# Retention without projections in between, a plain chunk of 256 tokens and passes of 512, output weights kept split

## Chip, cores, metric

One core of a Trainium2 chip. The metric is device time in microseconds of one execution of the program; the runs of the kernel before have a median of 917.03 us (915.97 to 918.96, three runs).

## What is computed

Retention over 4 batches, 8 heads, 576 positions, head size 64, then two feed-forward layers over the 2304 tokens of width 512. The second and third weights arrive as 64-bit floats and are converted on the chip.

```python
scores = (1 / sqrt(64)) * (q @ k.T)            # per batch and head
ret = scores * where(i >= j, gamma[h] ** (i - j), 0.0)
x = (ret @ v)  # -> (2304, 512), heads side by side

g = x @ w_gate                 # 512 x 1536
x = (g / (1 + exp(-g))) * (x @ w_val) @ w_out     # w_out 1536 x 512

r = maximum(x @ w_in, 0.0)     # 512 x 2048
out = (r * r) @ w_out2         # 2048 x 512
```

## The kernel before

All activations stay in one SBUF tile `xy` (128 x 4 x 2304). A float32 product is made as three TensorE matmuls: each operand is split by `split` into a rounded part (ScalarE cast, names ending in `_h` or `hi`) and a remainder (VectorE subtraction, `_l` or `lo`), and hi*hi, hi*lo, lo*hi are summed in PSUM (`three`, `product`).

**Retention** runs over 16 pairs (batch, two heads), `n` = 0 to 15, plus two iterations that only finish (`LAG` = 2). An iteration does `scores(n)` (tile `s`, masked by VectorE into `p_sb` and `pl`), `states(n)` (`kvs`, then a chain of three VectorE operations on `sb`), and `apply(n - 2)` (`o`, copied by ScalarE into `xy`). While it runs, `chain["on"]` ties every instruction to the one before it on its engine, so the written order is the order on the engine.

**Weights** come in units of 128 x 512 values. `conversion` loads a unit (`raw`, 512 KB), and `words` turns it into `w` with two ScalarE and four VectorE operations (two TENSOR_SCALAR, one SCALAR_TENSOR_TENSOR, one addition that the profile names CUSTOM_DVE_ANT_0). `pump` advances it a step at a time, `ensure` runs it until a unit is there. Before, each unit is stored to DRAM (`wst`) and read back (`w_in`, `wo`) where it is needed. 14 units are converted during retention.

**First layer, before.** Tokens 0 to 447 (`M0`) are a plain chunk: gate and value of the first six blocks (`hidden0`, 12 matmuls of 448 columns each) stand one behind each retention iteration from `n` = 6 to 17, their output products (`out0`, 72 matmuls, banks `a`) stand at the start of the first pass, and blocks 6 to 11 of the chunk form a small pass of their own (`"rest"`, 144 + 72 matmuls of 448). The other 1856 tokens go through two passes of two 464-token blocks. There, a pair of weight blocks and a pair of token blocks is multiplied with seven products instead of eight (`slot`, i = 1 to 7): the stationary operands `wi` are sums and differences of weight quarters (`stationary`, on GpSimd, split by ScalarE and VectorE, stored as `win` in the first pass and loaded in later ones), the moving operands `xo` are sums and differences of token blocks (`renew`, in place in `xy`). A system is one such set of 7 x 6 = 42 matmuls; a pass of the first layer has 12 systems (gate `g` and value `v` of six block pairs) and 288 output matmuls (`out1`, bank `oacc`, summed into `xy` by VectorE).

**Second layer.** Three passes of two 384-token blocks, 8 systems each (336 matmuls of 384 columns), and `out2`, 288 matmuls of 512 columns a pass.

After retention the order on the engines is set by the scheduler of the compiler layer, not by the written order.

In the profile nearly every operation has line L116, the line of the wrapper that issues it, so tiles tell the operations apart. Operations that the text speaks of: `p_sb`, `pl` at lines 405, `sb` 425, `renew` 540, `out0` 313, `hidden0` 294, `load_out` 713, the main loop 797.

Of the kernel before, what the change touches and what calls it, by code (L numbers as in the profile page):

```python
# [21 lines left out]
P = 128  # L22
# [17 lines left out]
HALF = F1 // 2  # L40
FROM = 6

LAG = 2

WA = 14

WARM = 3
UNITS_EARLY = 14

PUMPS = {0: 1, "out": 4}  # L50

PACE = 1.1
# [9 lines left out]
def retention_moe_kernel(  # L62
# [23 lines left out]
    early, parts = ExitStack(), ExitStack()  # L86
    ctx.enter_context(parts)
    ctx.enter_context(early)
    wa_p = pool(parts, "wa_p", WA)
    xs_p = pool(early, "xs_p", 4)  # L90
    t_p = pool(early, "t_p", 2)
# [11 lines left out]
    class Chained:  # L103
# [5 lines left out]
        def __getattr__(self, name):  # L109
            op = getattr(self.engine, name)  # L110

            def traced(*args, **kw):
                with ExitStack() as behind:
                    if chain["on"] and self.last is not None:
# [11 lines left out]
    units = {}  # L126
    order = [(1, what, f) for f in range(HALF) for what in "gv"] + [(1, "o", f) for f in range(HALF)]
    plain = len(order)
    for k in range(HALF // 2, F1 // 2):
        order += [(1, what, f) for f in (2 * k, 2 * k + 1) for what in "gv"] + [(1, "o", 2 * k), (1, "o", 2 * k + 1)]  # L130
    for k in range(F2 // 2):
        order += [(2, what, f) for what in "io" for f in (2 * k, 2 * k + 1)]
    raw_t, raw_flat, w_t = {}, {}, {}
    spare = []
    loads = {"next": 0, "pool": 0, "open": False, "cap": len(order) - 1}

    def prefetch(upto):

        while loads["next"] <= min(upto, len(order) - 1):
            i = loads["next"]  # L140
            if loads["pool"] < 2:
                loads["pool"] += 1
# [14 lines left out]
    wst = {u: part_p.tile([P, 512], F32, tag="w{}{}{}".format(*u), name="wst") for u in order}  # L157
    stored = set()

    def weight_tiles():  # L160
        return [wa_p.tile([P, 512], F32R, tag=x, name=f"w_{x}") for x in ("hi", "lo")]

    def finish(i):
        wf = w_t.pop(i).bitcast(F32)
        if i < plain:
            hi, lo = weight_tiles()
            split(hi, lo, wf)
            units[order[i]] = (hi, lo)
        sp.dma_start(out=wst[order[i]], in_=wf)
        stored.add(order[i])  # L170

    def words(raw, back, flat):
# [5 lines left out]
        wt = cv_p.tile([P, 512], U32, tag="w", name="w", bufs=3)  # L178
# [21 lines left out]
    def conversion():  # L200
        for i in range(len(order)):
            prefetch(max(i, min(i + 3, loads["cap"])))
            raw, back = raw_t[i]
            for n, wt in enumerate(words(raw, back, raw_flat.pop(i, None))):
                w_t[i] = wt
                if n == 2:
                    if i:
                        finish(i - 1)
# [3 lines left out]
            if back is None:  # L212
                loads["pool"] -= 1
            elif loads["open"]:
                spare.append(back)
            yield
        finish(len(order) - 1)
        yield

    def split(hi, lo, src):  # L220
        act.copy(hi, src)
        dve.tensor_tensor(out=lo, in0=src, in1=f32(hi), op=ALU.subtract)

    def stationary(w0, w1_, s1, to):
# [6 lines left out]
        yield  # L231
        yield
# [14 lines left out]
    def pump(k=1):  # L247
        for _ in range(k):
            if pumped["n"] < pumped["limit"]:
                pumped["n"] += 1  # L250
                next(convert, None)

    def ensure(key, where):
        while key not in where:
            pumped["n"] += 1
            next(convert)

# [11 lines left out]
    def split_x(cc):  # L269
        src = xy[:, cc, :M0]  # L270
        hi = xs_p.tile([P, M0], F32R, tag="xh", name="xh")
        lo = xs_p.tile([P, M0], F32R, tag="xl", name="xl")
        split(hi, lo, src)
        xs[cc] = (hi, lo)
# [7 lines left out]
    def cut(pair, a, n):  # L282
        return tuple(x[:, a:a + n] for x in pair)

    def project(f, what):
# [6 lines left out]
    hs, gates = {}, {}  # L292

    def hidden0(k):

        f, what = divmod(k, 2)
        ps = project(f, "gv"[what])
        yield
        if what == 0:
            gates[f] = t = t_p.tile([P, M0], F32, tag="t", name="t")  # L300
            act.activation(out=t, in_=ps, func=AF.Silu)
            return
        t = gates.pop(f)
        dve.tensor_tensor(out=t, in0=ps, in1=t, op=ALU.mult)
        yield
        hi, lo = (x[:, :M0] for x in weight_tiles())
        split(hi, lo, t)
        hs[f] = (hi, lo)

    acc = []  # L310
    part = part_p.tile([P, CC, M0], F32, tag="part", name="part")

    def out0(f):

        if f == 0:
            acc.extend(ps_a.tile([P, 512], F32, tag=f"a{i}", name=f"a{i}")[:, :M0] for i in range(CC))
        ensure((1, "o", f), units)
        w, h = units.pop((1, "o", f)), hs.pop(f)
        for cc in range(CC):
            three(acc[cc], cut(w, cc * P, P), h, f == 0, f == HALF - 1)  # L320
        if f < HALF - 1:
            return
        for cc, a in enumerate(acc):
# [598 lines left out]
```

## Time and profile before

| | us |
|---|---|
| median of three runs | 917.03 |
| the profiled execution, device time | 920.45 |
| its span in the trace | 918.7 |
| TensorE busy | 884.8 |
| VectorE busy | 679.3 |
| ScalarE busy | 438.6 |
| GpSimd busy | 103.3 |

The trace is that of the profiled execution; its device time is 1.75 us over its span and 3.4 us over the median. A matmul's recorded duration includes its way through the array; the rate of a row of matmuls is read from the distance of their starts. Three stages follow each other: retention up to 120.1 us, the first layer up to about 520 us (its end overlaps the second layer's start), the second layer to the end.

### The profile page before, as it was taken

To read this page: it belongs to the slowest core of one execution; us is meant where nothing else is said; L and a number is where in the kernel's file an instruction comes from. 1 tells how busy PE (TensorE), PEld (TensorE's weight loads), DVE (VectorE), ACT (ScalarE), POOL (GpSimd) and SP (SyncE) were. 2 spreads that over 40 slices of the span, in tenths; PEclk is the share of its full clock that TensorE was granted. 3 is DMA by queue.
4 is the path that set the end of the run, shared out by engine and by line. 5 is a ranking of instruction groups with operands and counts; after the bars stand their busy time and mean duration, and the time that the engine had idled before them with its cause. 6 is when DMAs were issued, how large, how long until landed. Compare 5 with 4: busy or idle time off the path is not lost.

```text
span 918.7 us, 13809 instructions
## 1 busy us (share of the span) xinstructions
PE 884.8 (96%) x5050; PEld 782.0 (85%) x5050; DVE 679.3 (74%) x1098; ACT 438.6 (48%) x781; POOL 103.3 (11%) x119
## 2 busy tenths in 40 slices
PE   7899959899999999899999999999999999999998
PEld 6688848788888899788888999989999999998986
DVE  3777887879989998877877899668754568554553
ACT  3555555675656655455543547534433334243220
POOL 2121160323303000000000223200000000000000
PEclk9999989899999999999999999999999999999999
DMA  8888557998879757889985457534664454554402
GB/s 327 280 277 292 160 196 234 358 318 283 296 258 305 277 190 252 261 302 330 317 289 194 152 200 253 199 140 148 204 197 127 160 171 161 171 184 155 141 3 69
DMA packets 83076, 202.85 MB, mean 221 GB/s; under 512 B 8512, under 2 KB 20288, under 8 KB 83008
## 3 DMA queue, kind: packets, MB, share of 16 engines
q1 hardware_dynamic: 83008, 201.97, 65.3%
q8 instruction: 40, 0.66, 0.3%
q14 instruction: 28, 0.23, 0.1%
HBM read 141.77 MB, written 60.16 MB: 220 GB/s over the span
## 4 chain that ended last, share of the span: by engine, by line
PE 71%; DMA 11%; DVE 10%; issue 3%; ACT 3%; POOL 1%; SPq 1%; ACTq 0%; DVEq 0%; POOLq 0%
PE oacc L116 29%; PE g L116 20%; PE v L116 11%; DMA raw<-in_w 6%; PE z L116 4%; DVE w L116 3%; PE o L116 3%; PE s L116 3%; DVE wi L116 2%; DMA w_in<-wst 1%; DVE xy L116 1%; DMA wst<-w 1%; DMA win<-wi 1%; DVE xo_l L116 1%; DMA kv_sb<-in_kv 1%
## 5 line engine op out<-in xcount | busy, mean ns | idle before, releaser
L116 PE MATMUL g<-xo_h,wi 128*128 128x464 f32 (+2 forms) x816 | 251.1, 359 | 9.4 <-ACT wi L116 3.3
L116 PE MATMUL oacc<-wo,ho_hi 128*128 128x512 f32 x576 | 181.0, 392 | 0.0
L116 PEld LDWEIGHTS g<-xo_h,wi 128*128 128x128 f32 x816 | 153.6, 190 | 23.9 <-ACT cbg L116 4.0
L116 PE MATMUL g<-xo_l,wi 128*128 128x464 f32 (+2 forms) x408 | 146.1, 358 | 0.0
L116 PE MATMUL v<-xo_h,wi 128*128 128x464 f32 (+2 forms) x432 | 136.8, 359 | 7.9 <-ACT wi L116 5.3
L116 PE MATMUL oacc<-ho_hi,wo 128*128 128x464 f32 (+1 forms) x432 | 138.5, 372 | 0.5 <-DVE xy L116 0.5
L116 PEld LDWEIGHTS oacc<-wo,ho_hi 128*128 128x128 f32 x576 | 107.3, 188 | 17.6
L116 DVE TENSOR_TENSOR xy<-oacc,xy 128x464 f32<-128x464 f32 (+2 forms) x146 | 94.3, 650 | 33.8 <-PE oacc L116 33.6
L116 PE MATMUL oacc<-wo,ho_lo 128*128 128x512 f32 x288 | 112.6, 392 | 0.0
L116 PEld LDWEIGHTS v<-xo_h,wi 128*128 128x128 f32 x432 | 80.8, 189 | 15.5 <-ACT wi L116 5.7
L116 PEld LDWEIGHTS oacc<-ho_hi,wo 128*128 128x128 f32 x432 | 81.0, 188 | 10.1 <-DVE xy L116 0.9
L116 DVE TENSOR_SCALAR w<-w 128x512 f32<-128x512 f32 (+1 forms) x136 | 58.6, 431 | 37.2 <-ACT w L116 36.4
L116 PEld LDWEIGHTS g<-xo_l,wi 128*128 128x128 f32 x408 | 77.7, 191 | 6.4
L116 PE MATMUL oacc<-ho_lo,wo 128*128 128x464 f32 (+1 forms) x216 | 80.1, 371 | 0.0
L116 ACT ACTIVATE raw<-raw 128x512 uint32<-128x512 uint16 x68 | 45.9, 675 | 68.6 <-DMA raw<-in_w 62.8
L116 PE MATMUL v<-xo_l,wi 128*128 128x464 f32 (+2 forms) x216 | 77.2, 357 | 0.0
L116 DVE TENSOR_TENSOR wo<-wo 128x512 fp32r<-128x512 f32 x78 | 54.2, 708 | 16.5 <-ACT wo L116 16.3
L116 DVE TENSOR_TENSOR cbg<-v,cbg 128x384 f32<-128x384 f32 (+1 forms) x72 | 41.7, 579 | 30.1 <-ACT cbg L116 19.4
L116 PEld LDWEIGHTS oacc<-wo,ho_lo 128*128 128x128 f32 x288 | 54.1, 188 | 11.5
L116 ACT CAST wo<-wo 128x512 fp32r<-128x512 f32 x78 | 47.4, 622 | 32.5 <-DMA wo<-wst 31.7
L116 ACT CAST wi<-w_in 128x512 fp32r<-128x512 f32 x72 | 44.1, 618 | 38.2 <-POOL w_in L116 9.2
L116 PE MATMUL z<-xo_h,wi 128*128 128x464 f32 (+1 forms) x192 | 61.8, 360 | 0.2 <-DVE cag L116 0.2
(100 smaller groups left out, 1366.6 us busy)
## 6 DMA issues: line engine op xcount, KB each, us to landing
wi<-win SPq DMA_DIRECT2D x84, 512.0 KB, 4.2
raw<-in_w SPq DMA_DIRECT2D x68, 512.0 KB, 5.0
win<-wi SPq DMA_DIRECT2D x60, 512.0 KB, 4.3
wo<-wst SPq DMA_DIRECT2D x78, 256.0 KB, 4.2
wst<-w SPq DMA_DIRECT2D x68, 256.0 KB, 5.2
w_in<-wst SPq DMA_DIRECT2D x52, 256.0 KB, 4.1
qk_sb<-in_qk SPq DMA_DIRECT2D x15, 576.0 KB, 5.8
kv_sb<-in_kv SPq DMA_DIRECT2D x15, 576.0 KB, 4.4
```

Of the source, the lines that this page charges most:

```text
L116: i = op(*args, **kw)
```

## The change

- Retention holds no projections. Instead it prepares the first pass: the operands of the first system (`operands`, one step per iteration from `n` = 6) and five of its seven moving operands (`chunks`, from `n` = 10), and the split of the plain chunk (`split_x`). A VectorE remainder is issued some steps behind its ScalarE cast (`behind`, `catch_up`). 7 units are converted there, not 14.
- The first layer's passes are two of 2 x 512 tokens. The plain chunk is 256 tokens (1024 to 1279) and is computed inside the first pass: each system has two `plain_slot`s of 12 matmuls of 256 columns, whose stationary operands are the quarters that the system has anyway and one more (`wb`); `out1` for it has 24 matmuls of 256 columns per block pair. `"rest"`, `out0` and the round trip of its partial sums through DRAM are gone.
- Units of the first layer are no longer stored in DRAM and read back: up to five (`HOLD`) wait in SBUF. Output weights are split once and kept split in DRAM (`wsp`, 512 KB a unit), later passes load both parts; in the first layer GpSimd makes the remainder.
- The second layer's passes take neighbouring token blocks; its matmuls are the same.

```diff
-M0 = 448
-M = {1: 464, 2: 384}
+M0 = 256
+M1 = 512
+T0 = 2 * M1
...
-    (1, 0): (M0 + M[1], M0 + 2 * M[1]),
-    (1, "rest"): (0,),
-    (1, 1): (M0, M0 + 3 * M[1]),
-    **{(2, p): (M[2] * p, NT // 2 + M[2] * p) for p in range(NT // (2 * M[2]))},
+    (1, 0): (0, M1),
+    (1, 1): (T0 + M0, T0 + M0 + M1),
+    **{(2, p): (2 * M[2] * p, 2 * M[2] * p + M[2]) for p in range(NT // (2 * M[2]))},
...
-HALF = F1 // 2
-FROM = 6
...
-UNITS_EARLY = 14
-
-PUMPS = {0: 1, "out": 4}
-
-PACE = 1.1
+UNITS_EARLY = 7
+HOLD = 5
+
+PACE = {(1, 0): 1.3, (1, 1): 1.3, (2, 0): 1.3}
...
-        sp.dma_start(out=wst[order[i]], in_=wf)
-        stored.add(order[i])
+        if i in w_t:
+            sp.dma_start(out=wst[order[i]], in_=w_t.pop(i).bitcast(F32))
+            stored.add(order[i])
...
-        for i in range(len(order)):
+        for i, key in enumerate(order):
+            while loads["held"] > HOLD - 1:
+                yield "held"
...
+            if key[0] == 1:
+                ready[key] = wt.bitcast(F32)
+                loads["held"] += 1
+            else:
+                w_t[i] = wt
...
+    behind = []
+
+    def catch_up():
+        while behind:
+            lo, src, hi = behind.pop(0)
+            dve.tensor_tensor(out=lo, in0=src, in1=hi, op=ALU.subtract)
+
     def split(hi, lo, src):
         act.copy(hi, src)
-        dve.tensor_tensor(out=lo, in0=src, in1=f32(hi), op=ALU.subtract)
+        behind.append((lo, src, f32(hi)))
+        if not chain["on"]:
+            catch_up()
...
+        to(4, a21)
...
-        ensure((1, what, f), units)
-        ps, w = bank(what)[:, :M0], units.pop((1, what, f))
-        for cc in range(CC):
-            three(ps, cut(w, cc * P, P), xs[cc], cc == 0, cc == CC - 1)
-        return ps
...
+        inputs[n] = [xs_p.tile([P, max(512, 2 * M0)], F32, tag="x", name="w_in")[:, :512] for x in range(2)]
+        for x, w in enumerate(inputs[n]):
+            ensure((ph, what, 2 * k + x), stored)
+            sp.dma_start(out=w, in_=wst[ph, what, 2 * k + x])
...
+        def to(x, src):
+            if x == 4:
+                if ph == 1:
+                    built[n, "p"] = w = wb_p.tile([P, 2, 256], F32R, tag="p", name="wb")
+                    split(w[:, 0], w[:, 1], src)
+                return
+            w = operand_tile(n, x)
+            split(w[:, 0], w[:, 1], src)
+            later.append((win[ph, k, what, x], w.bitcast(F32)))
...
-            if last:
-                bank = s_t[min(n + LAG, len(pairs) - 1)][:, 0, 256:256 + D]
-            else:
-                bank = ps_o.tile([P, 512], F32, tag="o", name="o")
+            bank = ps_g.tile([P, 512], F32, tag="gv"[last], name="o")[:, :D if last else 512]
...
+        def operands():
+
+
+            yield 6
+            load_in(0)
+            for _ in build(0):
+                yield 6
+
+        def chunks():
+            for i, step in ((1, 1), (5, 0), (5, 1), (6, 0), (6, 1), (2, 1), (7, 0), (7, 1)):
+                yield LAG + 2 * NP
+                renew((1, 0), i, step)
+            for cc in range(CC):
+                yield LAG + 3 * NP
+                split_x(cc)
+
+        begun = [[x, next(x)] for x in (operands(), chunks())]
+
+        def begin(n, which):
+            catch_up()
+            x = begun[which]
+            if n >= x[1]:
+                x[1] = next(x[0], 99)
...
-            fill = PUMPS[0] if n >= FROM - 2 else 0
...
+            fill = int(n > 2)
+            pump(2 * fill)
             if old:
                 apply(n - LAG, False)
-            pump(fill)
-            if LAG < n <= LAG + CC:
-                split_x(n - LAG - 1)
+            begin(n, 1)
             if new:
                 scores(n, (NC - 1,))
             pump(fill)
+            begin(n, 0)
...
-            if n == last + LAG:
-                apply(n - LAG, True)
-            if FROM <= n < FROM + 2 * HALF:
-                for _ in hidden0(n - FROM):
-                    pass
-            if old and n < last + LAG:
+            if n % 2:
+                begin(n, 1)
+            else:
+                catch_up()
+            if old:
                 apply(n - LAG, True)
             if nxt:
...
+        for x, _ in begun:
+            for _ in x:
+                catch_up()
+        catch_up()
+        pump(5 * UNITS_EARLY)
...
     def plain_slot(n, r):
 
         ph, p, k, what = systems[n]
-        ps = bank("gv"[r])[:, :M0]
-        product(n, ps, True, *(((1, 1), (2, 2)), ((7, 1), (4, 2)))[r])
+        ps = out_bank()[:, :M0]
+        for cc in range(CC):
+            w = built[n, ((1, 2), ("p", 4))[r][cc // 2]][:, :, cc % 2 * P:][:, :, :P]
+            three(ps, (w[:, 0], w[:, 1]), xs[cc], cc == 0, cc == CC - 1)
         if what == "g":
             if r == 0:
...
+                sys_[n]["c"] = gate_p.tile([P, 2, M0], F32, tag="gate", name="gate")
...
+        gc = sys_[n - 1]["c"]
+        tt(out=gc[:, r], in0=ps, in1=gc[:, r], op=ALU.mult)
         if r:
-            hidden(n, "a", ga)
+            hidden(n, "c", gc)
...
+    def load_out(n, fs):
+        ph, p = systems[n][:2]
         for f in fs:
-            ensure((ph, "o", f), stored)
-            w = wo_p.tile([P, 2, 512], F32R, tag="wo", name="wo")
-            sp.dma_start(out=w[:, 1].bitcast(F32), in_=wst[ph, "o", f])
-            act.copy(w[:, 0], f32(w[:, 1]))
-            tt(out=w[:, 1], in0=f32(w[:, 1]), in1=f32(w[:, 0]), op=ALU.subtract)
-            wos[f] = w
+            key = (ph, "o", f)
+            w = wos[f] = wo_p.tile([P, 2, 512], F32R, tag="wo", name="wo")
+            if p:
+                sp.dma_start(out=w.bitcast(F32), in_=wsp[key])
+                continue
+            if ph == 1:
+                ensure(key, ready)
+                src = ready.pop(key)
+                loads["held"] -= 1
+                act.copy(w[:, 0], src)
+                pool_e.tensor_tensor(out=w[:, 1], in0=src, in1=f32(w[:, 0]), op=ALU.subtract)
+            else:
+                ensure(key, stored)
+                sp.dma_start(out=w[:, 1].bitcast(F32), in_=wst[key])
+                act.copy(w[:, 0], f32(w[:, 1]))
+                tt(out=w[:, 1], in0=f32(w[:, 1]), in1=f32(w[:, 0]), op=ALU.subtract)
+            sp.dma_start(out=wsp[key], in_=w.bitcast(F32))
```

The order on TensorE in a retention iteration. Before, from `n` = 6 on (of the 12 matmuls of a projection the first three stand here):

```order
L116 MATMUL s<-qk_sb 128x128 x8
L116 MATMUL o<-qs,sb 64x128 x6
L116 MATMUL o<-p_sb,kv_sb 64x128 x8
L116 MATMUL s<-qk_sb 64x64 x2
L116 MATMUL kvs<-kv_sb 64x64 x8
L116 MATMUL v<-xh,w_hi 128x448
L116 MATMUL v<-xl,w_hi 128x448
L116 MATMUL v<-xh,w_lo 128x448
```

After, the same iteration:

```order
L106 MATMUL s<-qk_sb 128x128 x8
L106 MATMUL o<-qs,sb 64x128 x6
L106 MATMUL o<-p_sb,kv_sb 64x128 x8
L106 MATMUL s<-qk_sb 64x64 x2
L106 MATMUL kvs<-kv_sb 64x64 x8
L106 MATMUL o<-qs,sb 64x64 x2
L106 MATMUL o<-pl,kv_sb 64x64 x2
```

The projection is gone from the iteration, and nothing stands in its place on this engine.

The order on VectorE in the same stage, one iteration from one `p_sb` on. Before (`w_lo` is a weight's remainder, `raw` and `w` are conversion steps):

```order
L116 TENSOR_TENSOR p_sb<-s,mask_sb 128x1024
L116 ISA w<-raw,w 128x1024
L116 TENSOR_SCALAR w<-w 128x512
L116 TENSOR_TENSOR pl<-s,mask_sb 64x128
L116 TENSOR_TENSOR w_lo<-w,w_hi 128x512
L116 TENSOR_SCALAR w<-w 128x512
L116 SCALAR_TENSOR_TENSOR sb<-sb,qs_sb,kvs 128x64 x3
L116 SCALAR_TENSOR_TENSOR w<-raw,w 128x512
```

After, the iteration `n` = 14, the one with the most in it:

```order
L106 TENSOR_TENSOR p_sb<-s,mask_sb 128x1024
L106 TENSOR_SCALAR w<-w 128x512
L106 TENSOR_TENSOR xo_l<-xy,xo_h 128x1024
L106 TENSOR_TENSOR xy<-xy 128x2x512
L106 TENSOR_TENSOR pl<-s,mask_sb 64x128
L106 TENSOR_SCALAR w<-w 128x512
L106 SCALAR_TENSOR_TENSOR sb<-sb,qs_sb,kvs 128x64 x3
L106 SCALAR_TENSOR_TENSOR w<-raw,w 128x512
```

Two operations on the moving operands of the first pass (`xo_l`, `xy`) stand in the iteration, where a weight's remainder stood.

The order on TensorE where retention ends and the first pass begins. Before (`a` are the banks of `out0`):

```order
L116 MATMUL v<-xh,w_lo 128x448
L116 MATMUL a_1710<-w_hi 128x448
L116 MATMUL a_1710<-w_lo,w_hi 128x448
L116 MATMUL a_1711<-w_hi 128x448
L116 MATMUL a_1711<-w_lo,w_hi 128x448
L116 MATMUL a_1712<-w_hi 128x448
L116 MATMUL a_1712<-w_lo,w_hi 128x448
L116 MATMUL a_1713<-w_hi 128x448
L116 MATMUL a_1713<-w_lo,w_hi 128x448
L116 MATMUL g<-xo_h,wi 128x464
```

After:

```order
L106 MATMUL o<-pl,kv_sb 64x64 x2
L106 MATMUL g<-xo_h,wi 128x512
L106 MATMUL g<-xo_l,wi 128x512
L106 MATMUL g<-xo_h,wi 128x512 x2
L106 MATMUL g<-xo_l,wi 128x512
L106 MATMUL g<-xo_h,wi 128x512
L106 MATMUL z<-xo_h,wi 128x512
L106 MATMUL z<-xo_l,wi 128x512
L106 MATMUL z<-xo_h,wi 128x512 x2
L106 MATMUL z<-xo_l,wi 128x512
L106 MATMUL z<-xo_h,wi 128x512
L106 MATMUL oacc<-xs,wi 128x256 x6
```

The first system's products follow the last retention matmul directly, with the plain chunk's 256-column matmuls among them.

## Rows read from the trace of the kernel before

**Rows 1.** The page, its first line.

```profile
span 918.7 us, 13809 instructions
```

**Rows 2.** Busy time by stage: start:end, length, engines with instruction counts, clock, DMA.

```profile
0.00:120.10 120.10, 109.33 (x1306) 89.27 (x1306) 82.89 (x170) 63.72 (x142) 23.42 (x41) 0.97 0.79 267
120.10:180.00 59.90, 47.14 (x195) 39.25 (x196) 49.86 (x74) 33.85 (x63) 20.44 (x16) 0.86 0.76 253
180.00:300.00 120.00, 118.75 (x565) 105.39 (x564) 108.98 (x180) 74.37 (x131) 30.33 (x31) 1.00 0.87 297
300.00:400.00 100.00, 96.17 (x457) 86.39 (x456) 91.30 (x151) 53.05 (x85) 1.81 (x2) 0.98 0.76 255
400.00:520.00 120.00, 119.36 (x570) 106.56 (x569) 92.96 (x158) 62.12 (x105) 4.77 (x6) 1.00 0.76 262
520.00:640.00 120.00, 119.83 (x609) 109.59 (x609) 97.08 (x144) 60.65 (x107) 22.50 (x24) 1.00 0.55 191
640.00:914.00 274.00, 274.00 (x1357) 245.58 (x1355) 155.54 (x225) 90.83 (x153) 0.00 (x0) 1.00 0.45 145
```

**Rows 3.** What TensorE waited for, 118 to 185 us: total, times, longest.

```profile
PE v L116 <- ACT wi L116: 5.3, 1, 5.3
PE g L116 <- ACT wi L116: 3.3, 1, 3.3
```

**Rows 4.** Timeline of TensorE in retention and where it ends: start, length, operation.

```profile
18.90 1.16 PE L116 MATMUL s<-qk_sb 64*128 64x128 f32 x16
...
38.65 1.16 PE L116 MATMUL s<-qk_sb 64*128 64x128 f32 x16
...
59.61 1.16 PE L116 MATMUL s<-qk_sb 64*128 64x128 f32 x16
...
63.41 0.47 PE L116 MATMUL v<-xh,w_hi 128*128 128x448 f32 x1
63.71 0.36 PE L116 MATMUL v<-xl,w_hi 128*128 128x448 f32 x1
...
65.77 0.37 PE L116 MATMUL v<-xh,w_lo 128*128 128x448 f32 x1
66.07 0.33 PE L116 MATMUL s<-qs,sb 64*64 64x64 f32 x4
...
66.60 1.16 PE L116 MATMUL s<-qk_sb 64*128 64x128 f32 x16
...
120.18 0.47 PE L116 MATMUL a<-w_hi 128*128 128x448 f32 x1 [1.63 <-ACT xy L116]
```

**Rows 5.** Matmul starts at 384 and 512 columns, and TensorE's count at 464 columns.

```profile
646.17 0.34 PE L116 MATMUL g<-xo_h,wi 128*128 128x384 f32 x1
...
648.28 0.63 PE L116 MATMUL oacc<-wo,ho_hi 128*128 128x512 f32 x2
...
649.65 0.62 PE L116 MATMUL oacc<-wo,ho_hi 128*128 128x512 f32 x2
...
400.00:460.00 60.00, 60.00 (x288) 1.00 0.89 308
```

**Rows 6.** Groups by shape: busy us, mean ns, then idle time before.

```profile
L116 DVE TENSOR_TENSOR p_sb<-s,mask_sb 128x1024 f32<-128x1024 f32 x16 | 19.5, 1221 | 14.5 <-PE s L116 11.4 <-DMA mask_sb<-in_mask 3.1
L116 DVE SCALAR_TENSOR_TENSOR sb<-sb,qs_sb,kvs 128x64 f32<-128x64 f32 x48 | 13.4, 278 | 2.3 <-ACT sb L116 1.1
L116 DVE TENSOR_SCALAR w<-w 128x512 f32<-128x512 f32 x68 | 29.6, 435 | 36.7 <-ACT w L116 36.4
L116 DVE SCALAR_TENSOR_TENSOR w<-raw,w 128x512 uint32<-128x512 uint32 x68 | 48.1, 707 | 0.5
L116 DVE CUSTOM_DVE_ANT_0 w<-raw,w 128x1024 uint16<-128x1024 uint16 x64 | 44.9, 702 | 0.4
L116 DVE TENSOR_TENSOR wi<-w_in,wi 128x512 fp32r<-128x512 f32 x72 | 52.8, 738 | 3.1 <-ACT wi L116 2.8
L116 PEld LDWEIGHTS oacc<-wo,ho_hi 128*128 128x128 f32 x576 | 107.3, 188 | 17.6
```

More of the change, by code (lines that the diff above doesn't have):

```diff
@@ L113, in traced @@
                 with ExitStack() as behind:
-                    if chain["on"] and self.last is not None:
+                    if self.last is not None:
                         behind.enter_context(tc.issue_after(self.last))
@@ L123, in retention_moe_kernel @@
     pe, dve, act, pool_e, sp = map(Chained, (nc.tensor, nc.vector, nc.scalar, nc.gpsimd, nc.sync))
[L126 to L132, printed above, removed]
+    order = [(1, what, f) for k in range(F1 // 2) for what in "gvo" for f in (2 * k, 2 * k + 1)]
+    order += [(2, what, f) for k in range(F2 // 2) for what in "io" for f in (2 * k, 2 * k + 1)]
     raw_t, raw_flat, w_t = {}, {}, {}
-    spare = []
-    loads = {"next": 0, "pool": 0, "open": False, "cap": len(order) - 1}
+    spare, ready = [], {}
+    loads = {"next": 0, "raw": 0, "open": False, "cap": len(order) - 1, "held": 0}
     def prefetch(upto):
@@ L310, in retention_moe_kernel @@
[L310 to L321, printed above, removed]
-            return
-        for cc, a in enumerate(acc):
-            if cc % 2 == 0:
-                o = raw_p.tile([P, 1024], U32, tag="raw", name="part_sb").bitcast(F32)
-            dst = o[:, (cc % 2) * 512:][:, :M0]
-            act.copy(dst, a)
-            sp.dma_start(out=part[:, cc, :], in_=dst)
+    tt = dve.tensor_tensor
@@ L730, in out1 @@
         ph, p, k, what = systems[n]
-        m = M0 if p == "rest" else M[ph]
+        t0, m = (T0, M0) if which == "c" else (TOKENS[ph, p]["ab".index(which)], M1)
         o = out_bank()[:, :m]
@@ L783, in after @@
             return
[L784 to L792 removed]
+        if i in (1, 2, 3, 4, 5, 7):
+            for j in (5, 6) if i == 5 else (i,):
+                renew(passes[passes.index(at) + 1], j)
+    ho_p = pool(mid, "ho_p", 1)
+    gate_p = pool(mid, "gate_p", 1)
+    wo_p = pool(mid, "wo_p", 4)
     pace = {"due": 0.0}
@@ L820, in retention_moe_kernel @@
             load_out(*x)
-        if (n, p) == (systems.index((1, "rest", HALF // 2, "g")) + 1, "rest"):
-            sp.dma_start(out=xy[:, :, :M0], in_=part)
         for x in seq:
@@ L842, in retention_moe_kernel @@
                 wo_p = pool(ctx, "wo2_p", 8)
-            if 0 <= k < end and systems[k][1] != "rest":
+            if not 0 <= k < end:
+                continue
+            if isinstance(i, tuple):
+                plain_slot(k, i[1])
+            else:
                 slot(k, i)
-            elif i in ("s0", "s1"):
-                plain_slot(k, int(i[1]))
-            else:
-                k = end
             next(make, None)
-            if k < end:
-                if n < flip - 1:
-                    pace["due"] += PACE
-                    pump(int(pace["due"]))
-                    pace["due"] %= 1
-                after(k, i)
+            if n < flip - 1:
+                pace["due"] += PACE[ph, p]
+                pump(int(pace["due"]))
+                pace["due"] %= 1
+            after(k, i)
         for _ in make:
```

297 lines of the change are left out of this document (110 added, 187 removed).

## Prediction

> **What bounds the kernel now.** I read the busy time by stage first. From 180 us to the end TensorE is busy all but a few us [rows 2], so there only the number and width of its matmuls count. Two stages are different. In retention TensorE is busy too, but with two kinds of work: an iteration from 59.61 to 66.60 takes 6.99 us, of which the projection takes 66.07 - 63.41 = 2.66 and the retention itself 4.33 [rows 4]. Between 120.1 and 180 us TensorE is busy for 47.1 of 59.9 us, at 0.86 of the clock [rows 2]; it waits there for `wi`, once 5.3 and once 3.3 us [rows 3], the stationary operands of the first systems, which are started only when retention is over.
>
> To put numbers on it I need the time that a matmul takes in a row of them. Twelve of 384 columns stand between 646.17 and 648.28: 0.176 us each. Six of 512 stand between 648.28 and 649.65: 0.228. At 464, 286 starts (288 are counted, two reach in over the edge) fill 60 us: 0.210 [rows 5]. At 448, ten stand between 63.71 and 65.77: 0.206 [rows 4].
>
> After 120.1 us the kernel has 288 matmuls of 448 (72 of `out0`, 216 of the small pass), 1584 of 464, 1008 of 384 and 864 of 512: 59.3 + 332.6 + 177.4 + 197.0 = 766.3 us. TensorE ends at about 914 [rows 2], so the stretch has 793.9 us and 27.6 of them are lost. By stage: 195 matmuls of about 0.208 between 120.1 and 180 make 40.6, so 19.3 are lost there, and the rest mostly between 300 and 400, where the clock is 0.98 and TensorE is idle for 3.8 us [rows 2].
>
> **Part 1, retention loses its projections.** Its first three iterations are the same and end at 18.90 [rows 4]. Then come 13 iterations, `n` = 3 to 15. TensorE alone needs 4.33 each. VectorE has in them, by the order: 13 times the masking and states, 1.22 + 0.28 (`pl`, taken as a `sb`) + 3 x 0.28 = 2.34, together 30.4; seven conversions of 2 x 0.435 + 0.707 + 0.702 = 2.28, together 16.0; five remainders and three differences of 1024 elements at the 1.22 of `p_sb`, 9.8; five remainders of `wi` and `wb` at up to 0.74, 3.4 [rows 6]. That is 59.6, 4.6 per iteration, uneven: 6.4 in the fullest. So VectorE sets the rhythm by a little. DMA has about 23.4 MB to bring (16 pairs of 1.18, seven units of 0.52, tables); at 267 GB/s for a share of 0.79 [rows 2] a full queue would need 69 us, which is no bound but close enough to delay the first weight loads. The lower end for an iteration is VectorE's 4.6. The upper end is 6.6, what the iterations `n` = 3 to 5 of before took, (38.65 - 18.90) / 3 [rows 4]; they hold no projection either, but three loads of weights at once, and remainders that made `pl` wait. I take 5.35, the sum of each iteration's larger engine plus some 0.5 for waits, nearer to the engine sums because the remainders now come later. The last two iterations have no scores: 66.60 - 66.07 = 0.5 for the last chunk and about 1.8 for the others, 4.7 for both. Retention ends at 18.9 + 69.5 + 4.7 = 93, against 120.2 [rows 4]: **-27.1**, from -36 (4.6) to -11 (6.6).
>
> **Part 2, the matmuls after it.** 1584 of 512 instead of 464: 361.2. 432 of 256 columns instead of 288 of 448. The second layer is unchanged, 374.4. No row shows 256 columns. The line through 384 and 512 gives 0.176 - 128 x 0.00041 = 0.123; the widths 448 and 464 lie on it within 0.01, so I take it. From above it is bounded by 0.188, the recorded length of a weight load [rows 6], if loads went one after the other. At 0.123: 53.1. Sum 788.7, against 766.3: **+22.4**, to +50 at 0.188. This gives most of part 1 back, as the projections weren't removed but moved; only 6912 columns are saved. What makes it a gain is that retention's other engines had no work for 2.7 us of each iteration.
>
> The Trainium skill speaks against the narrow matmuls (TensorE: Matmul & The Clock Gate, "What overlaps and what doesn't"): a weight load overlaps a running matmul only in other row groups, and here every load takes all rows. By its load time of columns / 1.2 GHz (an estimate of 107 ns) a 256-column matmul would take 0.22 us and the sum would grow by 41 us. The trace disagrees at 512 columns: the rule would make 0.32 there, and the starts lie 0.228 apart [rows 5].
>
> **Part 3, the lost 27.6 us.** The first system's operands and five of seven moving ones are ready when retention ends, so the first product follows the last retention matmul. The first system and its plain slots hold TensorE for 24 x 0.228 + 24 x 0.123 = 8.4 us, the second system's begin brings 7 more; meanwhile VectorE has some 13 us of remainders and conversions for the second system (about 17 operations at 0.4 to 1.2 [rows 6]), and GpSimd two output-weight remainders ahead of the operand sums. That cover is thin: I leave 4 us. In the first pass I leave 4, what 180 to 320 lost at a similar VectorE load; for the change of passes, where the moving operands are single-buffered as before, 3. Together 11: **-16.6**, from -22 to 0.
>
> **Part 4, weights.** Per unit of the first layer the store and the read-back go; in the second and later passes the output weights come split, 512 KB instead of 256, without a cast and a remainder. From 640 us on DMA has a share of 0.45 and TensorE no idle time [rows 2], so this is off the path at both ends: 0. If the cover failed, each of the 44 later output units would show at most its remainder of 0.7 us [rows 6].
>
> Does VectorE fit into the first pass? Per block pair it has six conversions, 13.7; operand remainders of two systems, 2 x (3 x 0.74 + 2 x 0.54) = 6.6, taking 256 wide at 0.54, three quarters of 512; the recombination of eight 512-wide operations at 0.74 and three of 1024 at 1.22, 9.6; the plain chunk 1.5; the output sums 8 x 0.7 + 4 x 0.4 = 7.2. Sum 38.6 us, against TensorE's 132 x 0.228 + 72 x 0.123 = 39.0. Full on paper; but the seven early units and the first pair's sums, which are ScalarE copies, take off some 20 us over the pass, 92 percent then. Between 180 and 300 VectorE was busy for 109 of 120 us, 91 percent, and TensorE idle for 1.25 [rows 2].
>
> **Sum.** -27.1 + 22.4 - 16.6 = -21.3. The profiled execution, a span of 918.7 [rows 1] and 1.75 around it, ran 3.4 over the median; taken from the median of 917.03 I get **896**.
>
> **Rivals.** (A) Retention goes on at 6.6 us per iteration, since loads and ScalarE's waits for them set it and not the projections. For it: the three early iterations. Against: they had three weight loads in flight and a remainder ahead of `pl`. Price 13 x 1.25 = 16 us: 912. (B) VectorE becomes the bound of the first pass: at 38.6 of 39.0 in the middle pairs, any wait of VectorE is one of TensorE, and the units are now used straight from the conversion without a stock. If it works at 93 percent, six pairs take 6 x 41.5 instead of 234: +15, 911. For it: 300 to 400, with VectorE at 91 percent, lost 3.8 us and some clock [rows 2]. (C) Weight loads bind the 256-column matmuls, at `plain_slot` and the chunk's `out1`: 0.188 each, 432 x 0.065 = +28: 924, slower than before. It decides against the change from 0.123 + 21 / 432 = 0.172 on. Against it: at 384 columns the starts lie 0.176 apart, already less than the 0.188 of a load, so loads overlap each other or the matmuls. (D) A load and its matmul run one after the other, at the widths that the change brings: 0.188 + 0.123 = 0.31 at most, +81, up to 977; the 512-column starts at 0.228 leave no room for it [rows 5]. This is the page's rule above, which with its own load time would give 937.
>
> **How the numbers follow.** Forecast, 883 to 906: 0.62. A 0.12, B 0.14, C 0.08, D 0.02; 0.02 for something else. A and B vary by some us around their times and lie mostly below 914.3. The range takes in the forecast with its ends (retention at 87, less loss: 882) and A and B: 881 to 915. A measurement of this kernel can tell 0.3 percent, 2.75 us, from no change. Faster by more: 0.62 + 0.09 + 0.12 = 0.83. Within: 0.06. Slower: C, D and what is left, 0.11.
>
> **What will show it.** Retention's last matmul near 93 us, iterations of 4.4 to 6.5 us, the longest from `n` = 12 to 14. Starts of 256-column matmuls 0.12 apart; anything over 0.17 makes me wrong in sign. Between retention's end and 60 us later less than 6 us of TensorE waits, and a clock of 0.95 or more. VectorE at 90 to 95 percent in the first pass; if TensorE's waits there add up to over 10 us, released by `xy`, `wi` or `w`, it is B. The second layer's stretch, from its first 384-column matmul to the end, as long as before.

## Result

The changed kernel takes 904.97 us (median of four runs, 903.78 to 906.0), the kernel before beside it 916.55: a ratio of 0.9868 (95% interval 0.9846 to 0.989), 11.6 us faster. The forecast was 896, within 881 to 915: the sign and the range held, half of the gain came. The profiled execution of the changed kernel took 903.78 us; its line that answers to [rows 1]:

```profile
span 902.0 us, 13463 instructions
```

By stage, columns as in [rows 2] (start:end, length, then TensorE, weight loads, VectorE, ScalarE, GpSimd with their counts, clock, DMA share, GB/s):

```profile
0.00:86.60 86.60, 77.56 (x1162) 62.16 (x1162) 64.90 (x127) 43.72 (x105) 30.64 (x44) 1.00 0.85 306
86.60:146.00 59.40, 56.05 (x287) 46.60 (x283) 56.61 (x81) 41.26 (x78) 21.14 (x19) 1.00 0.65 228
146.00:206.00 60.00, 56.97 (x294) 47.64 (x294) 53.45 (x91) 37.46 (x72) 16.00 (x15) 1.00 0.63 209
206.00:266.00 60.00, 59.31 (x309) 49.84 (x308) 55.38 (x92) 31.93 (x58) 16.10 (x16) 1.00 0.60 206
266.00:330.00 64.00, 61.17 (x306) 50.57 (x305) 57.28 (x94) 35.08 (x56) 8.20 (x7) 1.00 0.80 271
640.00:890.00 250.00, 250.00 (x1239) 223.99 (x1238) 121.71 (x174) 67.75 (x111) 0.00 (x0) 1.00 0.54 174
```

Retention ends at 86.7 instead of 120.2, and the first product follows at once. The two long waits for `wi` [rows 3] and the clock of 0.86 behind them are gone. But from 86.6 to 330 TensorE is idle for 0.7 to 3.4 us in each row. The waits of TensorE there, 84 to 340 us (total, times, longest), are many short ones:

```profile
PE oacc L106 <- DVE xy L106: 3.7, 4, 1.6
PE z L106 <- DVE cav L106: 1.7, 1, 1.7
PE oacc L106 <- ACT xy L106: 0.9, 2, 0.5
PE oacc L106 <- ACT gate L106: 0.8, 2, 0.4
```

TensorE's timeline (start, length, operation) shows the iterations of retention, which answer to [rows 4], and the matmul rates, which answer to [rows 5]:

```profile
18.00 1.16 PE L106 MATMUL s<-qk_sb 64*128 64x128 f32 x16
...
22.32 1.16 PE L106 MATMUL s<-qk_sb 64*128 64x128 f32 x16
...
76.09 1.16 PE L106 MATMUL s<-qk_sb 64*128 64x128 f32 x16 [1.38 <-DVE p_sb L106]
...
86.40 0.34 PE L106 MATMUL o<-pl,kv_sb 128*64 128x64 f32 x4
86.66 0.50 PE L106 MATMUL g<-xo_h,wi 128*128 128x512 f32 x1
...
206.09 0.88 PE L106 MATMUL oacc<-xs,wb 128*128 128x256 f32 x6
206.80 0.88 PE L106 MATMUL oacc<-xs,wi 128*128 128x256 f32 x6
207.52 0.40 PE L106 MATMUL g<-xo_h,wi 128*128 128x512 f32 x1
```

From 18.00 to 76.09 lie twelve iterations, 4.84 us each; TensorE's own 4.33 is the distance of the first two. Six 256-column matmuls take 0.71 us twice, 0.119 each.

**Where the time went**, from trace to trace. A stretch's loss is the sum of the distances of matmul starts, less 0.2305 for each of 512 columns, 0.1755 for 384, 0.210 for 464, 0.206 for 448 and 0.1195 for 256; those of 256, 384 and 512 are what the traces give in undisturbed rows. The tail is what follows the last matmul.

| | before | after | change | forecast |
|---|---|---|---|---|
| retention ends | 120.2 | 86.7 | -33.5 | -27.1 |
| matmuls after it | 768.0 | 792.8 | +24.8 | +22.4 |
| lost after it | 25.9 | 17.8 | -8.1 | -16.6 |
| tail | 4.6 | 4.7 | +0.1 | 0 |
| span | 918.7 | 902.0 | -16.7 | -21.3 |

The medians give 11.6 and not 16.7, since the profiled run of before lies 3.9 us over its median and that of after 1.2 under its own. So two questions are left: why 18 us are still lost, and what the 5 us between 16.7 and 11.6 are.

### The profile page after: what moved, and what is told of

It reads as the page before. It is cut to its first block, busy times and chain, and to the rows that moved or that the text cites. A ratio compares the mean times of both kernels' runs of the same rounds, so it can differ in the third digit from the quotient of the medians.

```text
span 902.0 us, 13463 instructions
## 1 busy us (share of the span) xinstructions
PE 876.7 (97%) x5050; PEld 747.6 (83%) x5050; DVE 649.2 (72%) x1019; ACT 397.4 (44%) x708; POOL 120.5 (13%) x131
## 4 chain that ended last, share of the span: by engine, by line
PE 66%; DVE 15%; DMA 11%; issue 4%; ACT 3%; SPq 1%; POOL 1%; ACTq 0%; DVEq 0%; POOLq 0%
PE oacc L106 32%; PE g L106 17%; PE v L106 9%; DMA raw<-in_w 8%; DVE w L106 6%; PE z L106 4%; DVE xy L106 2%; PE o L106 2%; PE s L106 1%; DVE wi L106 1%; ACT w L106 1%; DVE xo_l L106 1%; ACT raw L106 1%; DMA kv_sb<-in_kv 1%; DMA qk_sb<-in_qk 1%
## 5 line engine op out<-in xcount | busy, mean ns | idle before, releaser
L106 PE MATMUL g<-xo_h,wi 128*128 128x384 f32 (+1 forms) x768 | 242.3, 366 | 3.2 <-ACT cbv L106 1.3
L106 PEld LDWEIGHTS g<-xo_h,wi 128*128 128x128 f32 x768 | 142.4, 188 | 24.5 <-ACT cbv L106 2.9
L106 PE MATMUL oacc<-ho_hi,wo 128*128 128x512 f32 (+1 forms) x480 | 152.1, 372 | 5.1 <-DVE xy L106 3.7
L106 PE MATMUL g<-xo_l,wi 128*128 128x384 f32 (+1 forms) x384 | 139.7, 364 | 0.0
L106 DVE TENSOR_TENSOR xy<-oacc,xy 128x512 f32<-128x512 f32 (+1 forms) x154 | 99.3, 651 | 47.9 <-PE oacc L106 47.5
L106 PE MATMUL v<-xo_h,wi 128*128 128x512 f32 (+1 forms) x384 | 124.7, 365 | 0.1
L106 ACT ACTIVATE raw<-raw 128x512 uint32<-128x512 uint16 x68 | 46.0, 677 | 124.8 <-DMA raw<-in_w 112.5
L106 DVE TENSOR_SCALAR w<-w 128x512 f32<-128x512 f32 (+1 forms) x136 | 65.4, 481 | 34.5 <-ACT w L106 33.5
L106 PE MATMUL oacc<-ho_lo,wo 128*128 128x512 f32 (+1 forms) x240 | 89.2, 372 | 0.6 <-DVE ho_lo L106 0.6
L106 PE MATMUL v<-xo_l,wi 128*128 128x512 f32 (+1 forms) x192 | 69.9, 364 | 0.0
L106 PE MATMUL z<-xo_h,wi 128*128 128x512 f32 (+1 forms) x192 | 62.4, 366 | 1.7 <-DVE cav L106 1.7
L106 ACT CAST ho_hi<-cbg 128x768 fp32r<-128x768 f32 (+1 forms) x36 | 32.6, 906 | 51.5 <-DVE cbg L106 51.5
L106 ACT COPY cbg<-g 128x384 f32<-128x384 f32 (+1 forms) x72 | 37.0, 514 | 39.3 <-PE g L106 39.1
```

## Experiments

Two theories for the loss. **Theory 1:** VectorE, busy for 92 percent from 86.6 to 266, is simply full; this is rival B. **Theory 2:** the weights' path. A unit is loaded into one of two buffers `raw`, two ScalarE casts and four VectorE operations turn it into `w`, and the last of them frees the buffer. Before, 14 units were converted when retention ended, now seven, of which two are used up by then; the rest is made on demand. The timeline of the changed kernel shows such a round and a TensorE wait beside it:

```profile
173.99 0.68 DVE L106 CUSTOM_DVE_ANT_0 w<-raw,w 128x1024 uint16<-128x1024 uint16 x1
...
174.70 4.32 SPq L106 DMA_DIRECT2D raw<-in_w  x2
...
176.14 0.68 DVE L106 TENSOR_TENSOR cbg<-v,cbg 128x512 f32<-128x512 f32 x1
176.74 0.68 DVE L106 SCALAR_TENSOR_TENSOR w<-raw,w 128x512 uint32<-128x512 uint32 x1
...
177.34 0.68 DVE L106 TENSOR_TENSOR xy<-oacc,xy 128x512 f32<-128x512 f32 x1
...
178.07 0.50 PE L106 MATMUL oacc<-ho_hi,wo 128*128 128x512 f32 x1 [1.61 <-DVE xy L106]
...
178.58 0.69 ACT L106 ACTIVATE raw<-raw 128x512 uint32<-128x512 uint16 x1 [4.78 <-DMA raw<-in_w]
```

The addition at 173.99 frees a buffer at 174.67; the load goes out at 174.70, and ScalarE, idle for 4.78 us, has it at 178.58. TensorE waits for a bank that `xy<-oacc` frees, which stands on VectorE behind a step of a weight. As this load does, all 31 loads from 146 to 330 us go out within 0.08 us of the addition that frees their buffer: a free buffer is what they wait for last.

What a late unit does to TensorE can't be read from a single gap, however. VectorE works almost without a pause ahead of this one; its last wait for a weight's cast had ended at 157.29. Ahead of the other two of the three largest gaps, at 105.0 and 298.6 us, it is the same: no such wait after 87 in the one case, none after 274.79 in the other. Kernels have to be compared.

**e1_after_again**: the changed kernel, as the others' measure.

> The changed kernel once more, unchanged, as the time that the others of this call are compared with. What is open: the sum from the profiled execution of before gave 16.7 us from span to span, the medians gave 11.6; the profile of before was 3.4 us over its median. If that is chance, the changed kernel's median is again about 905 and its TensorE losses after retention again 18 to 19 us, at the same places (256-column slots and the systems of the first pass). If the losses come and go from run to run, this trace has a different sum, by over 3 us.

904.94 us (903.06 to 906.27); before 916.73 beside it. Lost after retention: 19.5 us, with the same three large gaps (1.79 us at 105.9, 1.88 at 175.7, 1.71 at 298.3; in the first trace 1.82 at 105.0, 1.77 at 176.2, 1.71 at 298.6). The loss is no chance.

**e2_third_raw**

```diff
-    raw_p = pool(mid, "raw_p", 2)
+    raw_p = pool(mid, "raw_p", 3)
...
-            if loads["raw"] < 2:
+            if loads["raw"] < (2 if chain["on"] else 3):
```

> A third buffer for the loads of raw weights (after retention; three loads may be under way instead of two). Theory 1, VectorE: it is busy for 92 to 95 percent of the first pass and TensorE's waits there are for its operations on xy, cav and the gate; then the loads are not what is late, and the time stays within 1.5 us of the changed kernel's (905). Theory 2, the weights' path: ScalarE was idle for 112 us behind loads of raw, and the conversions that wait for them are what disturbs VectorE's order; then at least half of the 9 us that the first pass loses beyond the forecast come back, 900 or less, and ScalarE's idle time behind raw falls by over half. A rival of both: three loads at once take DMA share from wi and wo, +2 to +5 us.

895.07 us (892.13 to 899.45): 9.9 less than e1. The loss falls to 9.4 us. (The profiled run took 899.45, since its retention, at a clock of 0.83 in the first 20 us, ended only at 91.1.) Of the two signs of theory 2 one came, the time, and one did not: ScalarE's idle time behind loads fell only from 112.5 to 75.2 us, by a third and not by over half. The DMA rival falls.

**e3_sums_on_scalar**

```diff
-        if k == 0:
+        if k == 0 or p == 0:
```

> In the first passes of both layers the output products are copied by ScalarE and not added up over the block pairs, so most of the sum is left out: some 60 additions of 0.4 to 0.74 us, 35 to 40 us, go from VectorE in the first pass (some 6 us of 38.6 per block pair), and about as many copies go to ScalarE. The TensorE work is the same. Theory 1 (VectorE's load): the waits for xy and gate go, 6 to 9 us less than the changed kernel, 896 to 899, and the idle time of TensorE between retention's end and 330 us falls below 6 us. Theory 2 (loads of raw set the rhythm): VectorE gets idle and TensorE waits as before, within 2 us of 905.

908.03 us, 3.1 more. VectorE has 49.6 and 48.5 us of work from 146 to 206 and to 266 instead of 53.5 and 55.4, and TensorE loses more, 22.3. Its waits from 84 to 340 us have moved to the copies:

```profile
PE oacc L106 <- ACT xy L106: 3.0, 2, 2.2
PE z L106 <- DVE cav L106: 1.7, 1, 1.7
PE oacc L106 <- DVE gate L106: 1.6, 2, 0.8
```

With less work VectorE gave nothing back, which speaks against theory 1. It doesn't decide, since the copies now load ScalarE, which also makes the weights' casts: VectorE's wait for them, 86 to 340 us, rose from 12.1 to 17.9 us. In these kernels a full VectorE alone doesn't cost TensorE time, as e6 shows below.

**e4_prepare_late**: the generators `operands` and `chunks` yield 98 each time, so that all their steps run after the last iteration.

> The operands of the first system and its moving operands are not prepared during retention but after it. By my sum retention then gets shorter, by what the preparation costs its VectorE: six remainders at 0.5 to 0.74 and eight operations of about 1.2 are 13.6 us in the last nine iterations, of which the trace, TensorE-bound in eight of the 13 at 4.33, should give back only 3 to 6. Behind it TensorE waits for all of them: 13.6 us of VectorE and the load of the quarters, 14 to 18 us. Net +9 to +14, 914 to 919, as slow as the kernel before. If the preparation in advance was worth nothing (its place in retention costs what it saves), the time stays within 2 us of 905.

919.54 us, 14.6 more. Retention ends 4.8 us earlier (its last matmul starts at 81.7 instead of 86.5), twelve iterations take 4.50 each, near TensorE's 4.33, and the first product starts only at 88.28:

```profile
88.28 0.79 PE L106 MATMUL g<-xo_h,wi 128*128 128x512 f32 x1 [6.36 <-ACT xo_h L106]
```

The stretch behind it, columns as in [rows 2]:

```profile
86.60:146.00 59.40, 52.53 (x225) 42.02 (x226) 54.37 (x76) 38.98 (x69) 16.84 (x17) 0.81 0.48 178
```

The clock is back at 0.81 there, as it was 0.86 before. Preparing ahead costs 4.8 us and saves 19.

**e5_loads_other_queue**

```diff
-            sp.dma_start(out=raw, ...)
+            (sp if chain["on"] else pool_e).dma_start(out=raw, ...)
```

> Two buffers for raw weights as in the changed kernel, but after retention their loads are issued by GpSimd and no longer stand in SyncE's queue, where between 86 and 340 us the front instruction waits 64 us for the remainders wi and 98 us for w. A third buffer gave 9.9 us. Theory 2a, the queue: a load waits behind stores of operands whose remainders VectorE has not made yet, and the third buffer helped by letting a load be written ahead of them; then two buffers in a queue of their own give at least half of it too, 900 or less, with SyncE's stores unchanged. Theory 2b, the buffers: a load can't start before the addition that frees its buffer, whatever its queue; then the time stays within 2.5 us of 905. Rival to both: GpSimd's sums stand behind the waiting loads on its engine, operands come late, +3 us or more.

918.56 us, 13.6 more: the rival. GpSimd, 86 to 340 us, now stands at the loads (`raw`), and its sums for the operands behind them:

```profile
POOL raw L106 <- issue: 30.2, 9, 4.4
POOL raw L106 <- DVE w L106: 21.9, 8, 5.6
POOL raw L106 <- DVE xy L106: 17.7, 3, 8.3
```

SyncE's wait for `wi` grew from 64.3 to 106.3 us. A load whose buffer isn't free held up what stood behind it, and a queue of its own frees no buffer. What a queue on an idle engine would give wasn't tried.

**e6_third_raw_two_loads**: only the first line of e2's edit; in the program a load is written where it was, when one of two is done.

> Three buffers for raw weights, but a load is still written only when one of two is free, at the same place of the program as in the changed kernel. A load then finds a buffer that was freed one conversion earlier and waits for nothing at the front of SyncE's queue. Theory 2a (what stands behind a waiting load in the queue, or it behind others): most of the third buffer's gain without the third load, 895 to 900. Theory 2b in its strict form (what is needed is a load that is written one conversion ahead): within 2.5 us of 905.

894.27 us (893.75 to 895.42), ratio to before 0.9755 (0.9727 to 0.9782): the whole gain again. This is the fastest complete kernel of the study. But the edit didn't hold the third load back. After retention the scheduler sets the order, and this kernel's trace, of SyncE's loads and VectorE's additions, shows three units in the buffers:

```profile
151.58 3.58 SPq L106 DMA_DIRECT2D raw<-in_w  x2
...
167.76 0.33 SPq L106 DMA_DIRECT2D raw<-in_w  x1
...
171.84 0.68 DVE L106 CUSTOM_DVE_ANT_0 w<-raw,w 128x1024 uint16<-128x1024 uint16 x1
...
176.87 0.68 DVE L106 CUSTOM_DVE_ANT_0 w<-raw,w 128x1024 uint16<-128x1024 uint16 x1
```

The load at 167.76 goes out while the two units loaded before it still wait for their additions, at 171.84 and 176.87; so do all 31 loads from 146 to 330 us. So e6 repeats e2, and a third buffer without a third load was not tried. What SyncE's queue waits for, 86 to 340 us, hardly changed (`w` and `wi`: 98.1 and 64.3 us in the changed kernel, 107.1 and 54.4 here). What changed is the time that a unit may hold its buffer, from the load to the end of its addition: 12.2 us with two buffers, 17.7 with three, on average from 146 to 330. So what was short is the buffer. VectorE's wait at the front of its queue for a weight's cast, 86 to 340 us, first of the changed kernel, then of this one:

```profile
DVE w L106 <- ACT w L106: 12.1, 13, 1.9
```

```profile
DVE w L106 <- ACT w L106: 2.7, 6, 0.9
```

And this kernel's stages, columns as in [rows 2]:

```profile
206.00:266.00 60.00, 60.00 (x314) 51.21 (x313) 54.77 (x96) 32.25 (x59) 17.39 (x15) 1.00 0.62 215
266.00:330.00 64.00, 63.98 (x322) 53.62 (x321) 61.98 (x101) 36.23 (x57) 8.28 (x7) 1.00 0.85 293
```

In the last row VectorE is busy for 97 percent and TensorE waits for nothing: theory 1 in its plain form falls.

One doubt remained: each edit also lets the scheduler find another order. **e10_two_buffers_loads_twice** and **e11_three_buffers_loads_twice** make each load twice after retention, with two buffers and with the three of e6:

```diff
-            sp.dma_start(out=raw, ...)
+            for _ in range(1 if chain["on"] else 2):
+                sp.dma_start(out=raw, ...)
```

> Two buffers for raw weights, and after retention each load is made twice, one after the other into the same buffer, so a unit arrives some 3.9 us later (the median time from issue to landing) and 0.5 MB more per unit goes over DMA. Theory 2a: a buffer's round (load 3.9, two casts 1.35, four VectorE operations 2.28, and the queueing between them) sets how fast units come with two buffers; without queueing (3.9 + 1.35 + 2.28) / 2 = 3.8 us per unit, doubled 5.7, with six units needed per 39 us, 6.5 each; the queueing that left it short at two buffers stays. So the time grows a lot, by 15 to 50 us over 905, and VectorE's waits for w grow from 12 us to over 25. If the third buffer only gave the scheduler a luckier order, this run and the next grow by the same, under 10 us.

> Three buffers for raw weights (two loads under way, as in the run that took 894.3), and each load made twice. The same extra DMA traffic and the same extra waits at the front of SyncE's queue as with two buffers. Theory 2a: a round may take half as long again, so the doubled load fits nearly: 894 to 904, at least 10 us less than the two-buffer version. If traffic or SyncE's queue is what a longer load costs, and not the buffer's round, both versions grow by the same amount.

962.77 us (58 more than e1) and 907.2 (13 more than e6, 3 over what was expected). SyncE waits about as long for the first of two loads in both (74.9 and 77.8 us from 86 to 340), so its queue and the traffic don't make the difference of 56 us; the buffers do. But they make it in another place than that of the loss to be explained. Up to 400 us the kernel with two buffers loses 23.0 us and the one with three 21.7 (the changed kernel 17.4, e6 9.7): in the first pass a doubled load costs both, and the third buffer hardly helps. Between 400 and 640 the one with two buffers loses 49 us, the other 0.1; there the second layer starts short of units. So this pair shows what the buffers are worth at the start of the second layer; for the first pass e2 and e6 have to stand alone. TensorE's longest wait between 400 and 640, with two buffers:

```profile
PE oacc L106 <- ACT ho_hi L106: 27.2, 1, 27.2
```

VectorE's wait for `w` in the same kernel, 86 to 640 us:

```profile
DVE w L106 <- ACT w L106: 104.0, 46, 10.6
```

Put side by side, VectorE's wait for `w` from 86 to 640 us and TensorE's loss after retention nearly go together over five kernels, each with its own order:

| | wait for `w` | lost | time |
|---|---|---|---|
| three buffers (e6) | 13.4 | 8.9 | 894.3 |
| changed kernel | 29.6 | 17.8 | 905.0 |
| sums on ScalarE (e3) | 36.7 | 22.3 | 908.0 |
| three buffers, loads twice (e11) | 47.5 | 21.3 | 907.2 |
| two buffers, loads twice (e10) | 104.0 | 71.2 | 962.8 |

Others lie along the same line: e12 11.9 and 8.4, e2 13.8 and 9.4, e8 28.5 and 19.0, e7 39.2 and 30.1, e5 56.4 and 33.9. Two don't: e4, whose loss of 31.5 (wait 28.5) is in its late start, and the kernel before, whose VectorE waits 28.7 us for `w` from 180 to 640 while TensorE loses 7.7. The wait alone, then, doesn't make the loss.

An order's luck may move a time by some us. But with two buffers e1, e3 and e8 take 905 to 908, and with three e2, e6 and e12 take 894 to 898 (e4, e5 and e7 leave work out, move it or change a queue). That nothing but the buffer's round is at work isn't shown. Nor is it shown that the change made the buffers short: no run gave the kernel before a third buffer, or the changed kernel more units ahead.

**e7_no_plain_chunk**: `plain_slot`s and their `out1` are not issued, so the output of 256 tokens is left out.

> The plain chunk is left out: 432 matmuls of 256 columns, their gates and sums; the output for 256 tokens is missing. At 0.1195 apart (trace of the changed kernel) the matmuls are 51.6 us. If they and the gaps behind them (17 longer ones, 9 us together) are pure cost, the time is 844 to 853. If the narrow matmuls also cover something, waits for operands that TensorE would have shown without them, less comes back: 855 to 870, and TensorE's idle time in the first pass grows over the 18 us of the changed kernel. At the old rival's 0.188 apart, 81 us would go: 824.

863.6 us: 41.3 less, not the 51.6 of its matmuls, and the loss grows to 30.1. About 10 us of the narrow matmuls stand in for waits that TensorE would show without them. The 0.188 of rival C would have given 824.

**e8_output_weights_unsplit**

```diff
...
-                sp.dma_start(out=w.bitcast(F32), in_=wsp[key])
+                sp.dma_start(out=w[:, 1].bitcast(F32), in_=wst[key])
+                act.copy(w[:, 0], f32(w[:, 1]))
+                tt(out=w[:, 1], in0=f32(w[:, 1]), in1=f32(w[:, 0]), op=ALU.subtract)
...
+                sp.dma_start(out=wst[key], in_=src)
...
-            sp.dma_start(out=wsp[key], in_=w.bitcast(F32))
```

> Output weights are stored unsplit again, and every later pass splits them anew: a ScalarE cast of 0.66 us and a VectorE subtraction of 0.7 us for each of 44 units, 256 KB less to load per unit and to store per first-pass unit. My part 4 says 0: within 1.5 us of 905, since VectorE is busy for half to 80 percent of the later passes and DMA has room. If the cover fails, up to 44 x 0.7 = 31 us more; if the larger transfers of the changed kernel disturb the other loads, 2 to 5 us less.

905.22 us, 0.3 from e1. Keeping the weights split is worth nothing that these runs can tell.

**e9_before_again**: the kernel before once more.

> The kernel before, unchanged, for a second trace. Its first profile took 920.45 us, near the top of what its 17 runs in this study gave (913.28 to 920.32, median 916.7), and my forecast took the 3.4 us over the median as lying beside the change. If these 3.4 us are losses that come and go, a run nearer to the median shows less of them: fewer stretches under full clock in its first 180 us or shorter waits for wi, and retention's end or the loss behind it moves by about 3 us. If the profile itself costs them, the second trace has the same span within 1 us at the same clock.

918.15 us, span 916.4. Retention runs at a clock of 1.00 instead of 0.97 and its last small matmul starts at 113.1 instead of 115.7 us, while the loss, counted from there, is the same within 0.3 us:

```profile
0.00:120.10 120.10, 109.32 (x1318) 89.32 (x1319) 85.32 (x172) 65.98 (x146) 24.45 (x41) 1.00 0.79 269
120.10:180.00 59.90, 48.16 (x206) 40.43 (x205) 52.14 (x79) 35.03 (x64) 16.63 (x16) 0.89 0.80 273
```

So 2.6 of the 3.4 us by which the first profile lay over the median arose in its retention, all in two iterations between 24.5 and 38.7 us. The earlier one took 6.94 us instead of 5.82 here, with a wait of TensorE for `pl` of 2.31 us instead of 1.43. The later one took 7.20 instead of 5.61; right behind that wait the clock was at half (1.2 GHz, 0.50 from 32 to 34 us), where it was 1.00 here. This run is 0.5 over the median of before beside it (917.64).

**e12_chunk_384_passes_480**: e6 with `M0 = 384`, `M1 = 480`.

> With three buffers, a plain chunk of 384 tokens and passes of 2 x 480 instead of 256 and 2 x 512. By matmul starts: 1584 go from 0.2305 to 0.217 (the line through 384 at 0.1755 and 512 at 0.2305), 21.8 us less, 432 go from 0.1195 to 0.1755, 24.2 us more: 896.7, 2.4 over the version with 256. If the narrow matmuls were dearer than their starts say (weight loads, as in my rival C), the wider chunk would be the better one, by up to 10 us. If VectorE's load decides, its operations on 480 are shorter and those on the chunk longer by as much: no difference from 896.7 either way beyond 2 us.

897.85 us (895.79 to 899.08), 3.6 over e6 where 2.4 was worked out (2.6, if each is taken against the kernel before beside it). Starts at 480 columns lie 0.218 apart. Matmul starts price the split of tokens; the recorded lengths of weight loads don't.

## Why the prediction was right, and where it was off

**Sign and mechanism: right.** Retention was full with two kinds of work, and taking out one shortened it; the matmuls came back elsewhere at their price; the waits for `wi` went.

**Part 1, retention: 6.4 us too cautious.** The step that failed is 5.35 us per iteration, the larger engine's sum plus 0.5 for waits. Twelve iterations took 4.84; five of them stood at TensorE's 4.33. VectorE's 4.6 was an average over work that may slide between iterations, and what showed was mostly the preparation, 4.8 us in all (e4). Rival A (6.6 each) falls. In the trace of before, its three early iterations took 6.8 us more than three times 4.33: 4.7 are TensorE's waits for `pl`, 1.6 the stretch at half the clock.

**Part 2, matmuls: 2.4 too low.** The line through 384 and 512 gave 0.123 at 256 columns; 0.1195 was measured. 512 columns cost 0.2305 instead of 0.228, on 1584 matmuls 4 us. Rivals C and D fall by the starts: 12 matmuls in 1.43 us at 206.09, with loads recorded at 0.188 each. The page of the Trainium skill weighed there (TensorE: Matmul & The Clock Gate, "What overlaps and what doesn't") disagrees with this trace at 256 columns as it did at 512: loads that take all rows lie beside running matmuls. The 0.22 us that was worked out from it stands against 0.119 measured.

**Part 3, the loss: 8.1 us recovered, not 16.6.** This is the step that was wrong: the 4 us left for the first pass. The 4 us at the start held roughly (5.3 to 146 us), as did the change of passes (3.0 from 330 to 510); between 146 and 330, 9.7 us went instead of part of 4. I judged VectorE by its total, 92 percent, and asked whether it would be full. (By the sum's own terms, 231.6 less 20 of 234, it is 90; 92 was measured from 86.6 to 266.) It was as full with three buffers, 93 percent, and TensorE lost 2.5 us between 146 and 330. What the sum left out is the path that feeds VectorE: units are made on demand, a unit holds its buffer for 12.2 us, so two buffers give one per 6.1 us, and VectorE, with little to spare, stands 12.1 us at weights whose cast isn't done. With a third buffer that wait is 2.7 us, the loss is 8.9, under the 11 of the sum, and the time 894.3. That the buffers set this is shown by e2 and e6; the way from VectorE's wait to TensorE's, and the smaller stock as its origin, are argued. Rival B came nearest, with its 15 us instead of 7: that any wait of VectorE is one of TensorE and that units are used without a stock fits; that VectorE's own work is the bound does not.

**Part 4: right**, 0.3 us measured.

**The sum against a profile.** I took the 3.4 us between profile and median as lying beside the change, a term that was put at nothing without a reason. The after profile has its own offset, of the other sign; together 5.1 us of the forecast error. In numbers: 904.97 is 9.3 over 895.7; -6.4 from retention, +2.4 from matmuls, +8.5 from the loss (1.7 of it because the loss of before is 25.9 by these prices, not 27.6), +0.1 tail, +5.1 offsets, -0.5 because the median of before came out lower.

**What would show it**: 256-column starts and the clock came as said; the second layer's stretch, from its first 384-column matmul to the end, was 401.3 us instead of 398.4. The iterations took 4.32 to 6.26 us, but the longest was `n` = 7 and not one of 12 to 14. "TensorE's waits over 10 us, released by `xy`, `wi` or `w`: then it is B" was met by half: from 84 to 340 us they add up to 10.5, of which 5.1 are released by `xy` or `wi`. It would have named VectorE's load as the cause; e6 was needed.

## What to carry to other kernels

When work is moved out of a stage that had built up a stock, ask what will make the stock now, and follow one unit through its buffers: how long is a round from load to release, and how many rounds fit into the time in which a unit is needed. An engine's share of busy time doesn't answer that; its waits for its own inputs say more, and a further buffer is a cheap test. And compare two profiles only after asking how far each lies from its median.

## What the runs showed of the hardware

- Six 256-column matmuls of 128 rows start 0.119 us apart while each weight load is recorded at 0.188 us; 480 columns start 0.218 apart. The distance grows with the columns (256: 0.1195, 384: 0.1755, 512: 0.2305), and the recorded length of a load doesn't set it at these widths.
- A DMA that waits for its buffer held up GpSimd's arithmetic behind it when GpSimd issued it: 918.6 us against 904.9.
